# Small early loads gathered on the SP queue and a new hand-fixed instruction order, in a fused long-convolution and SwiGLU kernel

## The chip, the core and the metric

The kernel runs on one core of a Trainium2 chip. The metric is the device time of one execution in microseconds (us); lower is better. Engines are named as in the profile: PE multiplies matrices (PEld loads its weights), DVE and ACT work element by element, POOL does a few tiny operations, and SP only issues transfers. ACT and POOL issue transfers too. All transfers run on the same 16 DMA engines.

## The reference

What is computed, for 2048 rows of 640 channels (the FFN has 1728 hidden columns):

```python
k_shift = sum over t<4 of k_pad[:, t:t+S, :] * shift_k[:, 3-t]     # four-tap filter along the rows
kv  = k_shift * v
y   = irfft(rfft(kv, 2S) * rfft(ssm_k, 2S))[:S] + kv * ssm_D         # causal long convolution per channel
h   = x + layernorm(x) * y                                           # x is A_q
out = h + (silu(layernorm(h) @ w_gate) * (layernorm(h) @ w_up)) @ w_down
```

## The kernel before

**Tiling.** The 2048 rows are cut into four blocks `j` of 512, the channels into two halves `c` of 320. A block's convolution is done as matrix products with transform tables, and the FFN of a block follows when its `h` is complete. Names in the program carry `j`, `c` and a group `G` of the transform:

- `tapm`, `tap0`..`tap3` spread the four filter taps over the partitions. `hl..`/`he..` shift rows of `k` down for the filter, with the shift matrix `shm`. `kvm`, `kva`, `kvv` are the filter's multiplications and additions on DVE.
- `ktr0c` (PE, with the identity `ident`) and `kte0c` transpose the kernel `ssm_k`. For later blocks a transposing transfer `kx` and a shuffle `shk` do it.
- `s1X..`, `s1K..` and their evictions `e1..` are the first transform step of the signal (X) and of the kernel (K). `shX..G`, `shK..G` are transfers that shuffle partitions, `s2..`/`e2..` the second step. For block 0, three of the four transforms are done by one long product with the table `full` instead (function `dense`; here `s2K01`, `s2X00`, `s2X01`). The term with `ssm_D` enters as a product of one partition with the row `drow`, in `s1K00b0` and in `s2K01G0`..`G3`.
- `swB`, `swX`, `swC` are transfers that swap real and imaginary rows; `mr`, `mi` and further products on DVE multiply the spectra. `i2..G` and `e3..` are the first inverse step, `rs..G` the shuffle behind it, `i1..` the second inverse step.
- `q` and `hn` are the two layernorms, `o`, `h` the gate and the residual, `tr`/`te` (block 0) or the transposing transfers `hx` (blocks 1 to 3) turn `h` for the FFN. `gu` are the products with gate and up weights, `dn` those with the down weights.

**Order.** Nothing is scheduled at run time. The program is a list of 1219 operations (`Prog.op`). `Prog.replay` decodes the string `_ORDER`: for each operation an engine and a start value. The start values only sort the operations within each engine's queue, hand out buffers, and set two more things. The first is a count of *fillers* for PE: where the start values leave PE a gap ahead of an operation before the first `gu`, `replay` puts so many dummy products (`P.fill`, line 515 of the profile) into PE's queue, just ahead of that operation:

```python
gap = o.start - end - 0.25
o.lead = max(0, int(gap / 0.083)) if o.start > cold else max(0, int(gap / 0.166))
```

They always run, whether or not PE has to wait there. The second is that a transfer that would be issued more than one unit ahead of its start value is tied to an earlier ACT or DVE operation, so that it isn't issued much too soon. Apart from that every engine works through its queue in order, and an operation waits (by semaphore) for the data that it needs and for the buffer that it writes. An operation that waits holds back all behind it on its engine.

PE's queue before, around two places that matter here (fillers in brackets):

```
... s2K01G2, s2K00G1, [2] s2X00G3, s2X00G0, s2K00G2, s2X01G0, s2X01G1, s2K00G3, s2K01G3, i200G0, i200G1, s2X01G3, s2X01G2 ...
... [18] s2K10G0, [5] s2K10G2, i1010, s2K10G3, [3] s2K10G1, [2] s2X10G3, s1X11b1, [1] s1X11b3, i1011, s1K11b3 ... [19] tr00, [4] i210G1, gu001 ...
```

In code lines: L492 is every ordinary product, L515 the filler, L475/L478 the evictions and L501 the products and sums on DVE, L483 every plain transfer, L777/L778 the layernorm's scaling on DVE and on ACT, L520 and L514 the two memsets that DVE starts with. The second of these, `gpad`, writes the operand of the fillers; `P.warm` is its name in the code.

Of the kernel before, what the change touches and what calls it, by code (L numbers as in the profile page):

```python
# [43 lines left out]
class Prog:  # L44
# [61 lines left out]
    def replay(self, table):  # L106
        n = len(self.ops)
# [6 lines left out]
        for o in sorted(self.ops, key=lambda o: (o.start, o.idx)):  # L114
            for tl in o.tiles:
                if not tl.live:
                    pl = self.pools[tl.pool]
                    pl.free.sort(key=lambda f: f[0])
                    _, tl.base, tl.prev = pl.free.pop(0)
                    tl.live = True  # L120
            q = self.order[o.eng]
            o.pos = len(q)
            q.append(o)
            for tl in o.tiles:
                tl.touch.append(o)
# [211 lines left out]
def bass_sequential_preLN__ssm_conv_h3__swiglu_ffn__prompt_kernel(  # L337
# [31 lines left out]
    with ExitStack() as es:  # L369
# [18 lines left out]
        def V(t, off, n, p0=0, p1=128):  # L388
            return sb[p0:p1, t.base + off:t.base + off + n]
# [115 lines left out]
        def dram(apx, off, pairs):  # L505
            return bass.AP(apx.tensor, apx.offset + off, pairs)
# [580 lines left out]
        def block_j(j):  # L1087
            pb = 1000 * j
            if j == 0:
                load_kv_all(10)  # L1090
                load_full(11)
                tab_piece(2, oS1I, tab_np.shape[1], 30)
                tab_piece(0, 0, oS1K, 40)
                tab_piece(3, oS1K, oW2, 40)
                tab_piece(1, oW2, oS1I, 42)
                dma([(lambda: V(DROW, 0, D, 0, 1), lambda: dram(A_ssm_D, 0, [[D, 1], [1, D]]))], 1, [], [(DROW, 0)], 15, name="drow", eng="act")
            for c in range(2):
                if j:
                    load_kv(j, c, pb + 10 + 20 * c)
# [25 lines left out]

_INFO = None
_ORDER = (
    "c-pO030PBC7A7x`kdOtkhwLj^$i4sx*~tb3LLh`B2#6?%vRJFFindy}X>Bc4i+qk&#tpYBE|t1f9c|UNRIS#PDq2NtYf-0)wiPG1b!_X@nXmV}@0|0_yZ4-X"
    "{`=ntfDi~2h=Dv101AQ+ofrrRg+M_F2!g;<1Ny{!v?eOi0Y3J@fe!=rsX+8CS|?^;*(3A&EKepr$4cnH3*^y$qG1pUjcz^qfDa5b=Fxyafafz&JzxOvH|k+p"
    "=(8~Rb*~`!4F7SPPj&WG6nNCi<CgwBIq>|+A%Bp30KJE^9(sQbQs9FzKnCD}dKOB+A2#)$jCcUbQ|x%=gkRfwUhMv~B=CQfjN%A9Mils~5Pity=Rowo@a|dU"  # L1130
    "co+vj$m1p;{~Lb5?+O5qejC4u1AoXr;0gbtr5>UM{HcBxPD^4UF)JaFm;qS?xdN$z@PP_|2|Ws70+sPCG2cU+z*t~DZ~?%BI`DWb1@<AN4^|IpM7g1#K@Y@)"
    "AR@@Su|2UII0|f!<Hvp!TM8D#uE1YMyoTsS-bT_<+tI^;4FC*U58Vr$4xRxqus$FH{SsuvB4Wd_T~HL*2X%vIW0%D?!M=kB;-<#M!>7Xc!kvimu%BUK#A!rx"
    "{I&SiNG^(xtVeD|DiKo<Y4KI@Juo*s2tNtm5Z{Dyqb{S==t*cMx*ok9U6Y_mIE&em5W=p-9mMWQ>`QFJ+`vx5y+b;OuY!4Fcfhc5)o~}|vf+#2TyQFQBX(C@"
    "ZfpSNMRX#zB9_EAz(=F^qF=!5z#tR*6S5NLB{sw%;RW%%@%xd3P!VJgQjZj)M<wpZl5v%|d)NZpIoxdAQT%OuKH(cefH;x39P1=ZBJL;FkhYSpl9mxS5V0f*"
    "X%gu?$wj_RT1mb|9zu?gH<GuJ&yh<g4U{&DFlkKEJxmvA5<W~_OJBeik&tW{OV8RT=w{Cn9TFWBy&-8%dV%^fC4*X?1X8zAI+J!%ebkw>9NIoAg1(k+rb`*k"
    "%#T=KbB;4;tWxemRu{KlP$BH)mk7=a>y!PW@k|QiJ8l;DF0+<*m-jJG#qSiJN-h_y7nO)5Y$zunTEl*ubCz>lBolukX_QvUa#df;7RvLLe)S%;RdGP^qjIcj"
    "s``j{M~XpqL_SNk1cr&P1PQ1%v@BsV;uNYEGlv2}Yccl|P?$+b7`2)X#qJ?rV|UQMrVr)n5!d1GAb9cT;<d;X$bRI@apSOOuu4oH=5S&S_7>WL5#Z+F|AAxR"
    "C!u@Lqfp0C0rYBg5vm2H#H_{CV>%Ot<6H0(2_1xK37ZmhiPIBz6TeJE5;JgYQVsbS?jZR(B_nA@5}PuT0#Ntk;|Ws2M8dp88TJ#xZNdS9gSeP_g=(hlOxjKf"
    "Qafk>y^B7UzMD>EjN@+QuHgK_q3~Yk>G%qvfe-Q*@vrcmf-M4Ja!Yb4W(9_vP?sP~+?JStos2z<XOl*fwvgtNgQPanb|Q>qrS40rr*Ecdar<xpQB7Qgi^1E7"
    "qlhojjHH`1CH)5)gRZ2N)21;tGgeY5v=F18v5O969$^k;-DY{&vw5TVSNS2{0iIBBn47};fZNNBVHL5KvhJ|P@;>5}@|UqU@#_S?@XrcblVQRm!V$@zCeIbV"  # L1140
    "B1Ve)M0Rnv*e}tf?2(j8Orj=9w`5t$MCmo@dKpnlmyVUzN#{z5vhU?@$XXPO<svypK3P6q{+_&2L02{@<|v8EpR}{J2K5)J3A*iSK`KZ4fo6ZICT)rKXqrkd"
    "*Zfm$PyZ@yo#v+gvSD|IK7(LhX}V~9*DSV1Qa{vvZWwI%HnlN>Yr2@eM9;IVvE&)n*)(>e=@ny#In#XHL^Ch5Fzl~p@*JS+kmrJ9gj4K-dC*xkR-p}-33rq_"
    "I$g8e*`8j{xojM^pIk;BLD|S+ayDppqz_7+lBP(P=(F{Bqt(=7xNahuTg|!nW_%oB0U>$?DPR(s`U<s~UC0^5+0E%>Q#gwmy^K1(fqRZyB)r6=vh2*!%u?q2"
    "%$Y0=dkuf7V3;6IykF2KIL7A-E(kQqPT|<-O}N2J5cMScl8c2`g>Q*);#T2&F<dfEGCk$1l!-E5%7T=ODW9h-lYT3qDoRrLQoZO!(H8L~ak;cz%9Q2FVr2G|"
    "ZL*UxhD<5{n|!3=o?^42P`O4KqpDD?RmG&vSCKTjv|TEh<_pa#?O^R(-Om=4^;=_{xzXBbZLq^LH(GC5-Nsc$hV8fwY45i0rPb5nj55Y1hL`z1%fvY^*e&8n"
    "u1HVI+GHeoSh7q~A&)4WYPw>Iyj{*$1QZVG80j$idBs6hf+|jZUwujmSM5|fR0}kE-3oQT_Pkc7ou<2}hO1xFbm>;70%;Ygp|tk2*z|Sj7=4?$R^Jgl!TISP"
    "!+rgGh7U5_M!$ZG9%EQ-kQ(cZ%QH@7+%jxU?J)8(YBTyXVl5F%lkt?X%v5ZC-+aSrw9T-otxK)ftPWeDv)i)K^_Fdndz{T_Uv9r{w`PvXJeS##>31y5?6ONU"
    "8y)Qqg7c!I)-lF`aypzf&d;6QQF+sq;L33tow=@K&b!VEm*2h0HN%Z?AMy?HHRPSin~`7PyPZES2bD9^+njqRr#g@1qj@p8Tm0Gnw{zbt$O<0ySh6zm+ww`-"
    "R)1Q-)WY6EZBc8{Yk@;SOR+lpldPWLgkVL^{9<H?Txcpd5a=tcEkp-q7P&(ohjSx`BB;88;=`d(SQPo9c6;QrlC08COW9?aC4oU*gGx)w%9b;IiosH@w8T0&"
    "ZG=~wzc=qfJ~7YjUsQO~uPzV;t^_bedy9T#zssR<=W;E)cHZCBH?<}WKXqN|;<PF0RXS&y#9+<Pm@b*OSza(rG2bvR)E(DxObbj4%~DIM^^RqyGsX6{WtW9)"  # L1150
    "t+wuW+;+enX^wq1n{%f--?PGVBI{>Yde-bLcJ^1<f}Hl8#o1T0wK*79o$IDk<?8TU_7FUo9-^l*yC$2K1A4>WCEjg0cf7f|K;9i+W`26!)Vy8!DaF%+C4r=("
    "#^UwG?$9^ICyGuK%?X?haDuJDW5Ic0vNl_nm)@OTr*AXOx7WDVn|f>$?ai*ATulzOv)vYNAD#1#N9XIyD{^<aN4Z<wYqHK{DLk)w1ld32Ov#se|K;W8-p>hm"
    "FXl9PC*-cqZOpr$+nE=W*Xq0FGv^ok=H>hRs|tQBI1%VBP!<x4@ctIR+`rJzEqJlO?c3qI=08yIgFm^jvCv$!uP`gHIB+X~4i*QO1T%wkgWbV<!HVM3#e&e-"
    "(5etDd^WT;bRmQdRfOc>Vc{L&OX1RRFpQ4872X)05Sbm7oe@I`Cz2GQl#GtFM4|^+(qGb1q8+5IY^~fmOkBkoy1MFm#k7j%DxiAQkk_iK%V(F7E7lCYT;5WF"
    "9y)%gYxu_DcZX_fEQ61hpRTU2-Zi*n_@E&NhWLkF8tSS1au~O4OX*K#OUqKrCYCjpvuZZgY#nK+ZK}-}v2TQTWamh3ZCc%~y3O^e4YL}OYuDAf>krm58~zP&"
    "9!w_"
)


# [26 lines left out]
```

## Time and profile before

| | us |
|---|---|
| median of 6 runs | 310.94 |
| lowest and highest | 308.78, 313.08 |
| the profiled execution's own time | 311.48 |
| its span in the profile | 309.6 |

| engine | busy us | share | instructions |
|---|---|---|---|
| PE | 282.8 | 91% | 1765 |
| DVE | 234.7 | 76% | 406 |
| ACT | 186.9 | 60% | 280 |
| POOL | 27.0 | 9% | 34 |

PE's busy time holds the fillers too: 158 of them with 19.47 us. From about 206 us on, only FFN work of blocks 2 and 3 with the rest of block 3's convolution runs, and PE is busy throughout. The first 75 us, before the first `gu`, are different: PE has little real work there and depends on a chain through DVE, ACT and the DMA engines. How to read it: an engine's share over the whole span says little; a stage is bound by the wait that ends last in it.

### The profile page before, as it was taken

Reading aid. Unit: us, or ns where it says so; the run is one execution under the profiler, and the core shown is the slowest. Engines: PE = TensorE matmul, PEld = TensorE weight load, DVE = VectorE, ACT = ScalarE, POOL = GpSimd, SP = SyncE. Lnnn points to the kernel's source line nnn. Section 1 sums busy time; section 2 is a strip of 40 time slices with the busy share of each in tenths; the row PEclk is TensorE's granted clock in tenths of the full one; section 3 lists DMA queues with packets and bytes.
Section 4 is the critical chain, followed back from the end, with each engine's and each line's share of the span. In section 5 each row is a group of like instructions: output and inputs, shape, how many; then the busy total and the mean of one; then the engine's idle time right before and its main releaser. Section 6 shows DMA issues by size and latency. Waiting matters only on the chain.

```text
span 309.6 us, 4974 instructions
## 1 busy us (share of the span) xinstructions
PE 282.8 (91%) x1765; PEld 168.3 (54%) x1780; DVE 234.7 (76%) x406; ACT 186.9 (60%) x280; POOL 27.0 (9%) x34
## 2 busy tenths in 40 slices
PE   7999687779899989997999999979999999999992
PEld 4755365537555546774444566745555675444671
DVE  2896799769899988997999998896889973204222
ACT  3657577748768968674779975646797811250000
POOL 0021201122110011120000110200002010000000
PEclk9999999979999999999999999999999999999998
DMA  6958579669889987588671361445532122000021
GB/s 225 352 197 266 180 237 238 199 199 307 242 282 281 298 258 274 161 241 223 190 253 42 122 212 71 131 147 203 200 114 78 46 51 76 2 0 0 2 85 43
DMA packets 53116, 52.09 MB, mean 168 GB/s; under 512 B 21202, under 2 KB 46163, under 8 KB 53092
## 3 DMA queue, kind: packets, MB, share of 16 engines
q1 hardware_dynamic: 50274, 44.06, 44.4%
q0 software_dynamic: 1808, 6.93, 8.0%
q10 hardware_dynamic: 1010, 0.79, 0.8%
q8 instruction: 14, 0.23, 0.3%
q14 instruction: 10, 0.08, 0.1%
HBM read 19.00 MB, written 2.62 MB: 70 GB/s over the span
## 4 chain that ended last, share of the span: by engine, by line
PE 67%; DMA 11%; ACT 8%; DVE 6%; issue 3%; SPq 3%; POOL 0%; ACTq 0%; DVEq 0%
PE ps L492 62%; DMA sb<-sb 9%; ACT sb L475 5%; DVE sb L501 4%; PE ps L515 4%; SPq L483 2%; DMA sb<-in_A_ssm_D_dram 2%; ACT sb L478 1%; ACT sb L778 1%; ACT sb L790 1%; DVE stt L755 1%; DVE sb L777 0%; PE ps L624 0%; POOL stt L768 0%; SPq L981 0%
## 5 line engine op out<-in xcount | busy, mean ns | idle before, releaser
L492 PE MATMUL ps<-sb 128*128 128x320 bf16 (+3 forms) x1113 | 207.3, 336 | 2.6 <-DVE sb L501 1.6
L501 DVE TENSOR_TENSOR sb<-sb 128x1280 bf16<-128x1280 bf16 (+2 forms) x238 | 173.9, 767 | 16.5 <-ACT sb L475 4.8
L492 PEld LDWEIGHTS ps<-sb 128*128 128x128 bf16 (+2 forms) x1128 | 108.7, 98 | 83.1 <-issue 5.2
L475 ACT ACTIVATE sb<-ps 128x640 bf16<-128x640 f32 x131 | 88.7, 712 | 39.3 <-PE ps L492 38.6
L492 PE MATMUL ps<-sb,tab 128*128 128x320 bf16 x450 | 78.3, 304 | 11.2 <-DMA sb<-sb 7.2
L492 PEld LDWEIGHTS ps<-sb,tab 128*128 128x128 f16 x450 | 42.4, 99 | 39.2 <-DMA sb<-sb 8.1
L501 DVE TENSOR_TENSOR sb<-ps,sb 128x640 bf16<-128x640 f32 (+3 forms) x34 | 29.2, 858 | 42.4 <-PE ps L492 40.9
L1034 ACT ACTIVATE sb<-ps 128x1024 bf16<-128x1024 f32 (+2 forms) x32 | 29.3, 916 | 23.7 <-PE ps L492 23.6
L778 ACT ACTIVATE sb<-sb,stt 128x320 bf16<-128x320 bf16 (+1 forms) x34 | 24.0, 728 | 7.2 <-DVE stt L770 4.8
L478 ACT ACTIVATE sb<-ps 128x640 bf16<-128x640 f32 x31 | 21.0, 705 | 11.3 <-PE ps L492 11.3
L515 PE MATMUL ps<-sb 128*128 128x192 bf16 x158 | 19.5, 271 | 7.1 <-ACT sb L475 4.2
L755 DVE BATCH_NORM_STATS2 stt<-sb 128x6 f32<-128x320 bf16 x48 | 22.3, 483 | 0.2
L1050 ACT ACTIVATE sb<-ps 128x1024 bf16<-128x1024 f32 x18 | 18.4, 1024 | 5.6 <-PE ps L492 4.7
L515 PEld LDWEIGHTS ps<-sb 128*128 128x128 bf16 x158 | 14.3, 107 | 12.5 <-ACT sb L475 7.3
L768 POOL TENSOR_TENSOR stt<-stt 128x2 f32<-128x2 f32 (+1 forms) x10 | 11.4, 1138 | 53.2 <-DVE stt L766 42.7
L476 DVE CAST sb<-ps 128x640 bf16<-128x640 f32 (+1 forms) x8 | 6.2, 779 | 7.3 <-PE ps L492 7.3
L804 POOL TENSOR_TENSOR stt<-stt 128x4 f32<-128x4 f32 x2 | 2.6, 1298 | 77.9 <-DVE stt L802 77.9
L790 ACT ACTIVATE sb<-sb 128x640 bf16<-128x640 bf16 x8 | 6.0, 744 | 2.1 <-DMA sb<-in_A_q_dram 2.1
L797 ACT ACTIVATE sb<-sb,stt 128x640 bf16<-128x640 bf16 x8 | 6.6, 832 | 0.0
L777 DVE TENSOR_SCALAR sb<-sb,stt 128x320 bf16<-128x320 bf16 (+1 forms) x14 | 5.5, 395 | 0.9 <-DMA sb<-sb 0.5
L483 POOL DMA_DIRECT2D sb<-in_B_w_down_dram x3 | 2.1, 699 | 33.5 <-DVE sb L501 29.5
L483 POOL DMA_DIRECT2D sb<-in_A_k_dram x2 | 2.1, 1028 | 26.4 <-DVE stt L759 26.4
(30 smaller groups left out, 33.7 us busy)
## 6 DMA issues: line engine op xcount, KB each, us to landing
sb<-sb SPq DMA_DIRECT2D x144, 160.0 KB, 2.3
out_dram<-sb SPq DMA_DIRECT2D x16, 160.0 KB, 1.9
sb<-in_A_k_dram SPq DMA_DIRECT2D x4, 560.0 KB, 4.4
sb<-in_A_q_dram SPq DMA_DIRECT2D x3, 640.0 KB, 4.7
sb<-sb SPq DMA_DIRECT2D x24, 80.0 KB, 3.2
sb<-in_A_v_dram POOLq DMA_DIRECT2D x4, 320.0 KB, 4.6
sb<-in_A_k_dram POOLq DMA_DIRECT2D x2, 560.0 KB, 4.6
sb<-cst_full SPq DMA_DIRECT2D x1, 1024.0 KB, 8.8
```

Source lines behind the costliest of these rows:

```text
L475: fns = {"act": lambda a: a.activation(out=dst(), in_=src(), func=ACTF.Copy), "dve": lambda v: v.tensor_copy(out=dst(), in_=src())}
L478: fns = {"act": lambda a: a.activation(out=dst(), in_=src(), func=ACTF.Copy, scale=scale), "dve": lambda v: v.tensor_scalar(out=dst(), in0 ...
L483: fns = [(lambda g, d=d, s=s: g.dma_start(d(), s())) for d, s in subs]
L492: return lambda t: t.matmul(o(), l(), r(), start=st, stop=sp)
L501: return lambda v: v.tensor_tensor(out=o(), in0=a(), in1=b_(), op=op)
L515: P.fill = lambda t, pt: t.matmul(B32(pt, 1, 192), V(GUT, 13 * 512 + 256, 128), V(GUT, 13 * 512, 192), start=True, stop=True)
L755: vec(dve1(CW, False), lambda v: v.bn_stats(st6(l, j, b, c), V(xt, b * D + c * CW, CW)), [(xt, (b, c))], [(ST, ("s", j % 2, b, c))], prio, ...
L768: P.op({"pool": 0.95}, lambda g: g.tensor_tensor(out=y, in0=va, in1=stt[:, 288:288 + hi - lo], op=ALU.pow), c1 + [(ST, "half")], c3, prio, ...
L778: "act": lambda a: a.activation(out=dst(), in_=src(), func=ACTF.Identity, scale=rs(l, j, b), bias=tmv(l, j, 3)[:, b:b + 1])},
L790: P.op({"act": act_c(D) + 0.22}, lambda a, b=b, jt=jt: a.activation(out=V(jt, 0, D), in_=V(xt, b * D, D), func=ACTF.Copy, accum_out=tmv(l, ...
L1034: P.op({"act": act_c(n)}, lambda a: a.activation(out=dst(), in_=src(), func=ACTF.Silu), rd, wr, -1000, name=f"si{j}{i}")
L1050: P.op({"act": act_c(1024)}, lambda a: a.activation(out=V(ut, 0, 1024), in_=B32x2(u, 512), func=ACTF.Copy), [(u, 0), (u, 1)], [(ut, 0)], - ...
```

## The change

It has four parts. No operation is added or removed, except the dummy products.

1. **Loads.** `ident`, `shm`, `drow` (both times ACT before) and the first table piece `tab0` are issued by SP.
2. **`replay`** moves `gpad` to the head of DVE's queue, in front of `wpad`.
3. **A new `_ORDER`.** Every engine's queue is sorted anew, and 57 operations change their engine.
4. With it the count of fillers goes from 158 to 212.

```diff
@@ Prog.replay
+        q = self.order[self.warm.eng]
+        q.remove(self.warm)
+        q.insert(0, self.warm)
+        for i, o in enumerate(q):
+            o.pos = i
@@ the loads
-        dma([(lambda: V(IDN, 0, 128), ...)], 33, [], [(IDN, 0)], -2990, eng="act", name="ident")
-        dma([(lambda: V(SHM, 0, 128), ...)], 33, [], [(SHM, 0)], -2991, eng="act", name="shm")
+        dma([(lambda: V(IDN, 0, 128), ...)], 33, [], [(IDN, 0)], -2990, eng="sp", name="ident")
+        dma([(lambda: V(SHM, 0, 128), ...)], 33, [], [(SHM, 0)], -2991, eng="sp", name="shm")
...
-                tab_piece(0, 0, oS1K, 40)
+                tab_piece(0, 0, oS1K, 40, "sp")
...
-                dma([(lambda: V(DROW, 0, D, 0, 1), ...)], 1, [], [(DROW, 0)], 15, name="drow", eng="act")
+                dma([(lambda: V(DROW, 0, D, 0, 1), ...)], 1, [], [(DROW, 0)], 15, name="drow", eng="sp")
@@ the order
-    "c-pO030PBC7A7x`kdOtkhwLj^$i4sx*~tb3LLh..."
+    "c-pO#2UwHW8po6G3y_da_TGyuNJ0o?k_{w4AS93=..."
```

Decoded, the queues differ as follows.

The transfers at the start, each queue in its order:

```
            before                                             after
SP    taps, kin0, kraw00, x0, kraw01, full, vin0,     shm, taps, kin0, kraw00, ident, tab0, kraw01, full,
      tab1, kx10, shk10, swB010, shK00G3, swB000,     drow, x0, kx10, shK00G1, kin10, swB000, vin10, x1,
      swB001, swB011, rs00G1, kin11 ...               swB010, shk10, swB001, rs00G0, kin11, swB011 ...
ACT   shm, tab0, ident, drow, shK00G1, shK00G0,       vin0, shK00G0, shK00G2, tab2, shK00G3, rs00G1
      shK00G2, rs00G0
POOL  kin10, tab2, x1, vin10, tab3, vin11, kin20,     tab1, tab3, vin11, kin20, wg3, gul0, gul1, wd9,
      wg3, wg9, wu0, wu3, wd0, wd9, wdl, vin30,       wdl, vin30, x3
      vin31
```

SP's queue where block 0's second half is finished:

```
before  ... swX100, shK10G0, rs01G2, shK10G2, rs01G3, shK10G3, shK10G1, shk11, swB101, swX101, swB100 ...
after   ... swX100, shK10G0, rs01G2, shK10G3, shK10G1, rs01G3, shK10G2, wg9, shk11, swX101, swB100 ...
```

SP's queue where block 2's kernel is shuffled:

```
before  ... swX201, shK21G0, hx11, shK21G3, shK21G1, hx10, hx13, hx12, shX21G1 ...
after   ... swX201, hx10, shK21G1, hx11, shK21G0, rs20G1, hx12, st03, hx13, shX21G1 ...
```

PE's queue at the two places shown above:

```
after   ... [5] s2K00G3, s2K00G2, s2K01G2, s2X01G1, s2X01G0, s2X01G3, i200G0, i200G1, [21] s1X10b3, s2X01G2 ...
after   ... [15] i1010, s2K10G1, s2K10G2, [5] i1011, s2K10G3, [19] s1K11b1 ... [8] tr00, i210G1, gu000 ...
```

Where the fillers stand:

| PE's queue | before | after |
|---|---|---|
| up to the first `s2K01` product | 45 | 54 |
| from there to `i200G0` | 3 | 7 |
| from `i200G0` to the first `gu` | 110 | 151 |
| later | 0 | 0 |

The PE operations up to the first `s2K01` product are the same before and after, but for one product pair (`hl12`) that comes into this stretch; up to `i200G0` they are the same but for `s2X01G3`, which now stands before it; and up to the first `gu` they are the same.

On DVE and ACT, five of block 0's eight `q` scalings, `hn01`, `hn03` and the eviction `e300G2` move from ACT to DVE, `te01` and `he11` from DVE to ACT; later blocks exchange a dozen more in both directions. Between the product `mi0000` and the scaling `hn02`, DVE's queue holds 69 operations before and 79 after, both included but for `mi0000`.

## The prediction

> **What bounds the kernel now.** I read the page's engine and slice rows first, then busy time by stage, then the fillers of each stage, then the chain of work that ended last. The engine and slice rows:
>
> ```profile
> PE 282.8 (91%) x1765; PEld 168.3 (54%) x1780; DVE 234.7 (76%) x406; ACT 186.9 (60%) x280; POOL 27.0 (9%) x34
> ...
> PE   7999687779899989997999999979999999999992
> ...
> PEclk9999999979999999999999999999999999999998
> ```
>
> PE is the bound on average, and from slice 27 on in fact. But 91% includes dummy products, and slices 4 to 8 are thin. So I cut the span into five stages: A up to the first `s2K01` product, B to `i200G0`, C to the first `gu`, D to 205.88 us, E the rest. First PE, DVE and ACT, then the fillers (L515) alone:
>
> ```profile
> 0.00:15.49 15.49, 13.35 (x94) 9.64 (x95) 8.79 (x15) 8.20 (x11) 0.40 (x5) 1.00 0.88 289
> 15.49:33.53 18.04, 15.38 (x102) 8.96 (x101) 13.73 (x25) 10.96 (x17) 3.10 (x5) 1.00 0.69 238
> 33.53:74.65 41.12, 32.44 (x252) 21.31 (x253) 34.57 (x69) 29.01 (x46) 8.93 (x9) 0.96 0.75 220
> 74.65:205.88 131.23, 124.16 (x767) 74.07 (x776) 122.67 (x210) 98.00 (x147) 11.58 (x12) 1.00 0.67 204
> 205.88:303.75 97.87, 97.44 (x553) 54.31 (x558) 54.09 (x90) 40.77 (x61) 2.96 (x3) 1.00 0.21 73
> ...
> 0.00:15.49 15.49, 7.08 (x46) 5.53 (x46) 1.00 0.88 289
> 15.49:33.53 18.04, 0.41 (x3) 0.11 (x2) 1.00 0.69 238
> 33.53:74.65 41.12, 11.98 (x110) 8.68 (x110) 0.96 0.75 220
> ```
>
> The first figure is the stage's length, the second PE's busy time, the fourth DVE's. E has 0.43 us of idle PE: nothing to win. D has 7.07. In C only 32.44 - 11.98 = 20.46 us of 41.12 are real products, 8.68 us are idle. C is not PE's stage; a chain of DVE, ACT, SP and transfers sets it. The chain shows which transfers:
>
> ```profile
> 9.65 4.69 DMA sb<-in_A_ssm_D_dram
> ...
> 26.52 6.10 DMA sb<-sb
> 32.65 0.84 DVE sb L501
> ...
> 58.76 4.89 DMA sb<-sb
> ...
> 110.05 5.12 DMA sb<-sb
> ...
> 136.66 4.59 DMA sb<-sb
> ```
>
> These are `drow`, `swB000`, `shK10G1`, `shX20G1` and `shK21G1`: 4.6 to 6.1 us each, where the page's median shuffle takes 2.3:
>
> ```profile
> sb<-sb SPq DMA_DIRECT2D x144, 160.0 KB, 2.3
> ```
>
> PE waits 2.14 us for `i200G0` (`swB000`, then one DVE product), 2.43 for `s2K10G1`, 1.3 for `s2X20G1` and 1.75 for `s2K21G1`.
>
> **Part 1: the loads.** SP gets four more issues, some 0.4 us each (rows of SP's queue at the start: 0.35 to 0.48). They stand ahead of `x0` and `kx10`, which nobody needs before 11 us. In exchange `vin0` goes to ACT at once. Up to the end of `full` the same bytes move as before (`vin0`'s 640 KB in place of `x0`'s), so `full` still lands at about 4.14 + 8.8 = 12.9 us by its row; `kin0` and `kraw00` come later by what `vin0` took behind `full`, 14.5 - 12.9 = 1.6 us, so at 6.9 and 9.1. PE reaches their first users at 8.2 (1.2, 21 fillers 3.6, four `tapm` 2.2, 7 fillers 1.2) and, after four `hl` and 3 fillers, 10.7: hidden; without the fillers there it would cost up to 1.6.
>
> `drow` is where rule and trace part. [...] The row says that it took 4.69 us, to 14.34, together with `vin0`: the short queue got no turn. By the row it moves from 14.34 to about 13.0 (bounds: 7, if it passed all, 14.5 if it lands with `x0`). I take the row, 13.0: PE's 0.50 us of idle time in A goes, but PE is not there earlier (next part), so the loads alone are worth nothing.
>
> **Part 2: `gpad` first.** The fillers start after one DVE memset of 0.28 us instead of two: 1.2 instead of 1.64 us.
>
> **Parts 3 and 4 by stage**, lengths before and after.
>
> *A, 15.49.* PE's own queue is its length. Starts at 1.2; real products 13.35 - 7.08 = 6.27; `hl12` comes in, 0.5 at the slow clock; 54 fillers: 28 at 2.74/16 = 0.171 us, 9 at 2.31/16 = 0.144, 17 at 0.099, together 7.8; idle 0.3. Sum 16.1: **+0.6** (-0.4 to +1.6, `kraw00`).
>
> *B, 18.04.* Real products 14.97 - 0.27 (`hl12`) + 1.09 (`s2X01G3` now precedes `i200G0`) = 15.79; 7 fillers at 0.109, 0.76. Idle 2.66, of which 2.14 was `swB000`. SP issued it behind `shk10` (4 issues), `swB010` and `shK00G3`, and beside `x1` and `vin10`; now it stands behind `kin10` alone and ahead of these loads. PE has made its inputs at 16.1 + three `s2K01` at 1.8 + 1.1 + 0.55 = 23.2, ACT with evictions of 0.7 queued ahead of them at about 25; issued by 25.6, even at the old 6.10 it lands by 31.7, and with the DVE product at 32.5 it is within PE's 33.2. So 0.52 stays. Sum 17.07: **-1.0** (none: +1.2).
>
> *C, 41.12.* Real products 20.46, less 1.09 (moved to B), less the slow clock. The profile's clock rows:
>
> ```profile
> 62.29:65.70 3.41, 1.50 (x10) 0.76 (x11) 1.24 (x4) 1.52 (x3) 0.00 (x0) 1.00 0.70 241
> 65.70:69.11 3.41, 3.41 (x15) 1.60 (x14) 2.72 (x10) 1.70 (x3) 1.46 (x2) 0.50 0.60 159
> ```
>
> After a window with 1.50 us of PE work the next ran at half clock: 1.7 us lost. [...] Here the longest gap was 2.43. [...] I take the row: 17.67. Fillers 151 at 0.109: 16.4. Idle 8.68, less 2.43: `shK10G1` was the last of six shuffles on SP and met `wg3`; now it is issued before `rs01G3`, so when `i1010` can run it has landed, and `i1011` no longer stands behind `s2X10G3` and two `s1X11` products. That leaves 6.25; 41 more fillers, 4.5 us, may lie in waits that were idle; DVE, below, leaves room for 2.0 at most (17.67 + 16.4 + 6.25 is 40.3, its floor 38.3), and I take 1.5, leaving 4.7 (4.2 to 8.7). Sum 38.8: **-2.3**. What is late next is DVE. Its queue from `mi0000` to `hn02` grows from 69 to 79 operations: `e300G2` 0.82, `bn` 0.49, two `hn` 0.9, five `q` 1.4, four small 0.8, less 0.7; so 34.57 + 3.7 = 38.3. C can't be much below that, so I don't take more. ACT loses as much and has room (29.01).
>
> *D, 131.23.* `shK21G1` stood behind `shK21G0` (0.56), the transpose `hx11` (1.29) and `shK21G3` (0.59); now only `hx10` precedes it, while `shK21G0`, used just before, comes third: 1.4 of the 1.75 goes. `shX20G1` has as much PE work ahead as before (3 us): stays. PE's 1.59 at 205.88 is ended by DVE: stays. `wu0`, `wu3`, `wg9`, `wd0` go from POOL to SP at 0.6 us each, issued earlier; no use of them was waited for. Sum **-1.4** (-3.4 to +1).
>
> *E*: 0.
>
> **Sum**: +0.6 - 1.0 - 2.3 - 1.4 = -4.1, so 311.48 becomes 307.4 in the profiled execution. Against the median of the runs, 310.94, that is **306.8**. One per cent, 3.1 us, is about what a measurement of this kernel can tell from no change.
>
> **Rivals.**
>
> *Same: a collision replaces the one removed.* POOL now issues `kin20` and `wg3` back to back, over 1 MB, ahead of `rs01G2` and `rs01G3`, which lead to `i1010`. If those take 4.9 instead of 2.3, C gets 2.6 back and the half clock's 1.7: +0.2, 311.1. For it: DMA share 0.75 in C, and `wg3` did this before. Against: 15 fillers ahead of `i1010` keep PE busy.
>
> *Slower: the fillers are paid in full.* They run whether or not PE waits. 54 more cost 5.5 us, over 5 of them in B and C. If no wait there goes and the half clock stays, B is 15.79 + 0.76 + 2.66 = 19.2 and C 19.37 + 16.4 + 8.68 = 44.5: with A's 0.6 that is +5.1, **316.0**. It decides (slower by 1%) from where less than 2 us of waits is saved. For it: already before, fillers are followed by waits, as if they stood in the wrong places. Against: the transfers that ended the longest waits are those moved forward.
>
> *More*: all idle time in C that fillers can cover goes, and D's waits too: A -0.4, B -1.0, C down to DVE's 38.3 (-2.8), D -3.4: 303.3.
>
> *The loads do nothing* by themselves is my own assumption above; it alone decides no sign.
>
> **Chances.** Forecast 0.50 (it spreads, so 0.12 of it lies within 1%), same 0.19, slower 0.21, more 0.10. Faster by over 1%: 0.38 + 0.10 = 0.48; within 1%: 0.31; slower: 0.21. Range 301.5 to 314: down to the "more" case with a margin, up through "same" and into the slower one. The likeliest's own: 303 to 310.
>
> **What would show it.** Right: the first `s2K01` product at 15.5 to 16.5; `drow` landed near 13; `i200G0` at 32.5 to 33.5 with no wait over 0.5; no half clock near 66; the first `gu` at 70 to 73; `s2K21G1` waiting under 0.6; 212 fillers with about 25 us. Wrong: the first `gu` at 75 or later with more filler and no less idle time (the slower rival), or an early `gu` whose gain D gives back in waits for weights or shuffles.

## The result, and the profile after

The changed kernel takes 309.37 us (median of 29 runs, 306.45 to 311.97), the kernel before, run beside it, 312.37 us (64 runs). The ratio is 0.9914, 95% interval 0.9892 to 0.9936; a second series of the same two (e1 below) gave 0.989 (0.9859 to 0.9921). Medians are of all runs; the ratios count only the fast ones, those within 1.5% of the fastest of their kernel. So about 3 us are gained, where 4.1 were forecast, and not where they were forecast. The profiled execution of after took 310.75 us, 0.73 less than that of before; one lies above its median and the other below, so 2 us of the gain can't be seen in this pair of profiles.

First the page of after, engine and slice rows:

```profile
PE 287.9 (93%) x1819; PEld 173.8 (56%) x1834; DVE 235.9 (76%) x413; ACT 184.4 (60%) x273; POOL 22.6 (7%) x29
...
PE   8899988587899998998999999999999999999993
...
PEclk9799999879999999999999999999999999999999
```

PE has 54 matmuls more, all fillers. The half clock that stood in slice 8 of before is still there, now over two slices, and a second one has come in slice 1. Then the same table by stage: length, PE, PEld, DVE, ACT, POOL, granted clock, DMA share. The last row holds what were D and E (131.23 + 97.87 = 229.10 us before). Below the dots are the fillers alone (L520 now):

```profile
0.00:16.88 16.88, 14.39 (x105) 10.31 (x105) 10.04 (x15) 8.00 (x11) 1.15 (x7) 0.90 0.95 261
16.88:34.04 17.16, 16.70 (x113) 10.04 (x114) 15.39 (x27) 10.05 (x16) 0.00 (x0) 1.00 0.72 235
34.04:78.75 44.71, 35.31 (x287) 25.42 (x286) 35.49 (x75) 26.09 (x40) 7.09 (x7) 0.92 0.75 222
78.75:303.77 225.02, 221.51 (x1319) 128.02 (x1332) 174.14 (x299) 140.27 (x208) 14.35 (x15) 1.00 0.48 149
...
0.00:16.88 16.88, 7.21 (x54) 5.80 (x54) 0.90 0.95 261
34.04:78.75 44.71, 17.03 (x151) 13.22 (x151) 0.92 0.75 222
```

A grew by 1.4 us, B shrank by 0.9, C grew by 3.6 (44.71 instead of 41.12), and all behind it shrank by 4.1. In this pair of profiles that adds up to nothing: the last product ends at 303.77 us after and at 303.75 before. The 0.7 us by which the profiled execution of after is shorter lie behind the last product. Part of them is the end of the program, where SP waits once for every semaphore that a transfer has used. When the last output has landed, 43 semaphore instructions of SP are left in before and 36 in after, and the span ends 2.96 and 2.52 us later. It ends 2.46 to 2.53 us later in all profiles with after's order up to the first `gu`, 2.96 to 3.02 in all with before's. No step of the prediction counted that.

C has no less idle PE than before: 44.71 - 35.31 = 9.40 us, against 8.68, although its fillers went from 11.98 to 17.03 us. The chain of work that ended last, by start, length and what, shows where they lie:

```profile
1.61 6.80 DMA sb<-in_A_k_dram
...
34.60 0.71 ACT sb L483
35.32 0.05 issue
35.36 1.91 PE ps L520 x21
...
52.06 6.65 DMA sb<-sb
...
63.04 1.46 PE ps L520 x8
...
65.04 1.78 PE ps L520 x15
...
70.62 1.74 PE ps L520 x19
```

Between 35 and 77 us fifteen pieces of this chain are fillers, 13.9 us of the 17.0. In before they were ten, 8.6 of 12.0. The pattern, as at 35 us: an eviction on ACT ends, 0.05 us later fillers start, and the product stands behind them. And 52.06 is the shuffle `shK10G0`, issued between `kin20` (51.23) and `wg3` (52.18): 6.65 us, with PE waiting for `s2K10G0`.

### The profile page after: what moved, and what is told of

Read it like the earlier page. It is cut to its first block, busy times and chain, and to the rows that moved or that the text cites. A ratio compares the mean times of both kernels' runs of the same rounds, so it can differ in the third digit from the quotient of the medians.

```text
span 308.9 us, 5073 instructions
## 1 busy us (share of the span) xinstructions
PE 287.9 (93%) x1819; PEld 173.8 (56%) x1834; DVE 235.9 (76%) x413; ACT 184.4 (60%) x273; POOL 22.6 (7%) x29
## 3 DMA queue, kind: packets, MB, share of 16 engines
q0 software_dynamic: 960, 3.41, 4.0%
## 4 chain that ended last, share of the span: by engine, by line
PE 75%; DMA 8%; ACT 7%; DVE 5%; issue 2%; SPq 1%; ACTq 0%
PE ps L497 69%; DMA sb<-sb 5%; PE ps L520 5%; ACT sb L480 5%; DVE sb L506 4%; DMA sb<-in_A_k_dram 2%; SPq L488 1%; ACT sb L1039 1%; DVE stt L760 1%; ACT sb L483 0%; ACT L1039 0%; PE ps L993 0%; PE ps L629 0%; ACT sb L1055 0%; DVE sb L484 0%
## 5 line engine op out<-in xcount | busy, mean ns | idle before, releaser
L497 PEld LDWEIGHTS ps<-sb 128*128 128x128 bf16 (+3 forms) x1128 | 109.0, 98 | 83.9 <-issue 4.3
L480 ACT ACTIVATE sb<-ps 128x640 bf16<-128x640 f32 (+1 forms) x134 | 90.7, 714 | 44.6 <-PE ps L497 42.0
L520 PE MATMUL ps<-sb 128*128 128x192 bf16 x212 | 25.1, 272 | 7.6 <-ACT sb L480 6.0
L520 PEld LDWEIGHTS ps<-sb 128*128 128x128 bf16 x212 | 19.6, 108 | 14.7 <-ACT sb L480 11.2
L483 ACT ACTIVATE sb<-ps 128x640 bf16<-128x640 f32 x29 | 19.5, 702 | 10.6 <-PE ps L497 10.5
L783 ACT ACTIVATE sb<-sb,stt 128x320 bf16<-128x320 bf16 (+1 forms) x26 | 19.1, 754 | 3.9 <-DVE stt L775 3.2
L481 DVE CAST sb<-ps 128x640 bf16<-128x640 f32 x6 | 4.8, 820 | 4.9 <-PE ps L497 4.7
L782 DVE TENSOR_SCALAR sb<-sb,stt 128x320 bf16<-128x320 bf16 (+1 forms) x22 | 7.9, 379 | 0.1
L764 DVE BATCH_NORM_AGGREGATE stt<-stt 128x2 f32<-128x12 f32 x24 | 4.3, 195 | 0.0
L488 POOL DMA_DIRECT2D tab<-cst_tab x2 | 1.3, 634 | 36.9 <-ACT sb L480 26.5
```

The costliest lines, as they stand in the source:

```text
L480: fns = {"act": lambda a: a.activation(out=dst(), in_=src(), func=ACTF.Copy), "dve": lambda v: v.tensor_copy(out=dst(), in_=src())}
L483: fns = {"act": lambda a: a.activation(out=dst(), in_=src(), func=ACTF.Copy, scale=scale), "dve": lambda v: v.tensor_scalar(out=dst(), in0 ...
L497: return lambda t: t.matmul(o(), l(), r(), start=st, stop=sp)
L782: "dve": lambda v: v.tensor_scalar(out=dst(), in0=src(), scalar1=tmv(l, j, 5)[:, b:b + 1], scalar2=rs(l, j, b), op0=ALU.add, op1=ALU.mult),
L783: "act": lambda a: a.activation(out=dst(), in_=src(), func=ACTF.Identity, scale=rs(l, j, b), bias=tmv(l, j, 3)[:, b:b + 1])},
```

## The experiments

Each was timed against the kernel before on the same chip; the ratio is to that. "First `gu`" is the end of the first `gu` product in the profile of that kernel, "behind it" the time from there to the last product's end. e17 has two runs only, and so no ratio.

| kernel | fillers | first `s2K01` starts | `i200G0` ends | first `gu` | behind it | DVE operations done at first `gu` | median us | ratio (95%) |
|---|---|---|---|---|---|---|---|---|
| before | 158 | 15.49 | 34.26 | 75.38 | 228.35 | 107 | 312.37 | 1 |
| after | 212 | 16.88 | 34.58 | 79.30 | 224.48 | 114 | 309.37 | 0.9914 (0.9892-0.9936) |
| e1 after again | 212 | 16.70 | 34.39 | 78.00 | 225.08 | 114 | 308.59 | 0.989 (0.9859-0.9921) |
| e2 after, 28 cut | 184 | 16.54 | 34.24 | 76.08 | 225.98 | 114 | 307.98 | 0.9879 (0.9818-0.994) |
| e3 after, `wg3` late | 212 | 16.58 | 34.28 | 75.19 | 224.62 | 114 | 306.54 | 0.9857 (0.9808-0.9907) |
| e4 before, then after | 158 | 14.54 | 32.13 | 75.91 | 227.56 | 107 | 311.22 | 0.9965 (0.9933-0.9997) |
| e5 e3, 63 cut | 149 | 17.00 | 34.69 | 74.34 | 224.44 | 114 | 306.55 | 0.9846 (0.9792-0.9899) |
| e6 e3, 151 cut | 61 | 16.49 | 34.18 | 72.15 | 224.32 | 114 | 305.42 | 0.978 (0.9719-0.9841) |
| e7 before, loads on SP | 158 | 17.01 | 33.63 | 74.47 | 227.98 | 107 | 312.48 | 1.0043 (1.0012-1.0073) |
| e8 e5, `vin0` later | 133 | 15.38 | 33.91 | 72.91 | 228.43 | 112 | 308.34 | 0.9867 (0.9815-0.992) |
| e9 after, 151 cut | 61 | 17.72 | 35.42 | 71.89 | 224.68 | 111 | 303.77 | 0.9759 (0.9719-0.9799) |
| e10 before, 110 cut | 48 | 14.86 | 33.23 | 72.18 | 228.77 | 108 | 306.68 | 0.9866 (0.9822-0.9911) |
| e11 after, then before | 212 | 18.59 | 36.29 | 78.51 | 225.28 | 115 | 312.81 | 0.9992 (0.996-1.0025) |
| e12 e6, `vin0`, `wdl` | 45 | 17.11 | 35.08 | 76.30 | 226.76 | 115 | 307.58 | 0.9816 (0.9764-0.9868) |
| e13 before, `vin` later | 158 | 15.61 | 34.54 | 76.03 | 226.95 | 107 | 311.38 | 1.0004 (0.9973-1.0035) |
| e14 before, `shK21G1` | 158 | 15.55 | 33.72 | 75.98 | 227.52 | 107 | 311.03 | 0.9981 (0.994-1.0022) |
| e15 after, 191 cut | 21 | 14.39 | 31.92 | 69.20 | 226.81 | 111 | 302.20 | 0.9724 (0.9675-0.9774) |
| e16 e15, `wdl` early | 21 | 14.11 | 31.64 | 69.95 | 225.21 | 114 | 302.73 | 0.9692 (0.9638-0.9745) |
| e17 as e11 | 212 | 17.21 | 34.90 | 75.77 | 226.28 | 115 | 312.06 | none |
| e18 before, 73 cut | 85 | 15.68 | 33.33 | 70.94 | 229.26 | 107 | 308.46 | 0.9914 (0.9883-0.9946) |

Stage marks of one profile scatter by a us or two; the ratios are the firmer column.

### Is the split typical, and what are fillers worth? (e1, e2, e9, e10, e15)

e1 is the changed kernel again.

> The changed kernel once more, to learn whether the profile of it shown above is typical: its first gu started at 78.75 us, 3.9 us later than before, and everything behind it took 225.0 us instead of 229.1. If this split belongs to the order, the second profile shows the first gu at 77.5 to 80, the half clock near 60 again, and a time of 309.0 to 309.8. If the late transfers near 52 us were chance, the first gu starts at 74 to 77 and the time is one to three us shorter in that execution.

The split belongs to the order: 78.00, then 225.08 us.

Fillers are set by each operation's `lead`. e2 sets three of them to 0:

```
         for o in self.order["pe"]:
+            if o.name in ("s2X10G3", "i1010", "i1011"):
+                o.lead = 0
```

> The changed kernel without the 8, 15 and 5 fillers ahead of s2X10G3, i1010 and i1011 (28 of 212; the chain of after charges 1.46 and 1.78 us to them). Theory F (fillers are paid: transfers had made PE late, so the planned gaps no longer exist): the first gu comes 2.5 to 3 us earlier, near 76, and the time falls to 307 to 308. Theory T (the transfers set these products, the fillers lie in waits): PE waits instead of running fillers, the first gu stays within 1 us of 78.7, the time within 0.5 us of the changed kernel.

The first `gu` came at 76.08, 1.9 us before e1 and 3.2 before after: theory F. The ratio can't be told from that of e1.

e9 takes all 151 of C away (from `s1X10b3` on), e10 the 110 of before (from `i200G0` on):

```
+        on = False
         for o in self.order["pe"]:
+            on = on or o.name == "s1X10b3"
+            if on:
+                o.lead = 0
```

> The changed kernel without the 151 fillers between i200G0 and the first gu, wg3 where the change put it, directly behind kin20. With wg3 moved as well the first gu ended at 72.15 us and the ratio was 0.978. Theory F (fillers are most of the loss): first gu at 72.5 to 74, ratio 0.979 to 0.984. Theory T (the collision is most of it): shK10G0 takes over 6 us as in after, s2K10G0 waits 3 us or more, first gu at 75 to 77, ratio 0.985 to 0.99.

> The kernel before without its 110 fillers between i200G0 and the first gu; all else as before. Theory F: those too are paid; the first gu ends 2 to 4 us before 75.38, the time falls to 308.5 to 310 (ratio 0.988 to 0.995). Theory W (before, the stage waits for shuffles with or without fillers): first gu at 74.5 to 75.5, ratio 0.996 to 1.004.

Theory F in both, and past its own figure: 0.9759 after, 0.9866 before. In each order the fillers of C cost about 1.3%, 4 us. Without their 17.03 us C of after, from the end of `i200G0` to that of the first `gu`, fell from 44.72 to 36.47: half of them came back. Of the other half, 6.4 us went into the real products (busy 24.67 us instead of 18.29) and 2.4 into waits (11.80 us instead of 9.40). The clock did what it was feared to do: its granted share in this stretch was 0.86 instead of 0.92. Engine and clock rows of e9:

```profile
PE 278.8 (92%) x1668; PEld 160.9 (53%) x1683; DVE 235.7 (78%) x413; ACT 184.6 (61%) x273; POOL 22.6 (7%) x29
...
PEclk9999999579999999999999999999999999999998
```

More of C is at half speed than in after, and the kernel is the faster for it all the same.

e15 leaves only the 21 fillers ahead of the first product:

```
+        for o in self.order["pe"]:
+            if o.name != "tapm":
+                o.lead = 0
```

> The changed kernel with only the 21 fillers ahead of the first product left (191 cut: 151 in C, 33 in A, 7 in B). Theory F: the 33 and 7 are paid as well in part; the first s2K01 product starts at 14.5 to 15.5 instead of 16.7 and the ratio is 0.970 to 0.975, under the 0.9759 with the 151 cut. Theory C (near the start they hold the clock up): half clock from 8 to 15 us, the first s2K01 product at 16.5 or later, ratio 0.976 to 0.982.

Theory F again: first `s2K01` at 14.39, 2.5 us before after's, and 302.20 us. Its ratio and that of e9 overlap; that the 40 in A and B cost something is shown by the mark alone.

### What does `wg3` behind `kin20` cost? (e3, e5, e6)

```
+        for o in self.ops:
+            if o.name == "wg3":
+                o.start = 54.5        # was 47.38; behind shK10G2
```

> The changed kernel with the weight load wg3 no longer directly behind kin20 on POOL but after shK10G2 (seven shuffles later). Theory T (collision): shK10G0, which took 6.65 us from issue to landing, takes 3 to 5; the wait of 2.9 us for s2K10G0 falls under 1, the first gu comes 2 to 3 us earlier, the time is 307 to 308. Theory F (fillers): only the wait goes, the fillers behind it stay in PE's queue and i1010 is reached little earlier; the first gu moves by under 1 us, the time by under 0.5 us.

The chain of e3 at the same two places:

```profile
51.76 5.22 DMA sb<-sb
...
61.47 1.24 PE ps L524 x15
...
66.51 1.74 PE ps L524 x19
```

`shK10G0` takes 5.22 instead of 6.65 us, the four shuffles issued between 55.8 and 57.8 take 2.1 to 2.2 each instead of 2.3 to 3.0. The first `gu` came at 75.19, 2.8 to 4.1 us earlier, and this profile has no half clock in C:

```profile
PEclk9799999999999999999999999999999999999999
```

Theory T, for the marks; the ratio, 0.9857, overlaps with e1's. The product behind the 15 fillers still waits for them.

> The changed kernel with wg3 behind shK10G2 and, besides, without the 63 fillers from s2K10G0 to the first gu (149 of 212 stay). With wg3 moved alone the first gu ended at 75.19 us and everything behind it took 224.6 us. Theory F (these fillers lie on PE's path, since PE and ACT's evictions take turns there and a filler comes between them): the first gu ends at 71.5 to 73, the time is 303.5 to 305.5. Theory T (the shuffles of the next half, shk11 above all, landed at 66.3 us, and the evictions set the end of the stage): the first gu stays at 74.5 or later, 306 to 307. Theory G (the lead is given back behind the first gu, because the loads of weights come no earlier): the first gu ends near 72, but 226 to 228 us follow, 305.5 to 307.

First `gu` 74.34, ratio 0.9846: nearer to theory T. Of 63 fillers cut on top of `wg3`, 0.9 us came back; the profile has half clock where e3 had none.

> The same, but with no filler at all between i200G0 and the first gu (61 of 212 stay). Theory F: PE is nowhere slowed by a dummy product, the first gu ends at 70 to 72, the time is 302 to 304.5. Theory C (the fillers hold the clock): with some 20 us of real products in 40 us several windows of 3.41 us at half clock appear, each worth up to 1.7 us; the granted clock of the runs falls from 0.99 to under 0.985, the first gu ends no earlier than with 63 cut, the time is the same or higher.

72.15 and 0.978, granted clock 0.9725 on average in its six runs: the clock fell as theory C said, the time fell as theory F said. It can't be told from e9 (0.9759), where `wg3` stands as in after: with the fillers gone `shK10G0` was issued 0.2 us ahead of `kin20` in e9, instead of 0.8 behind it, and took 3.18 us. The collision was a matter of the fillers as much as of the place of `wg3`.

### The loads at the start (e7, e8, e12)

e7 is part 1 alone: before, with `shm`, `taps`, `kin0`, `kraw00`, `ident`, `tab0`, `kraw01`, `full`, `drow`, `x0` on SP and `vin0` on ACT at the times of after:

```
+            if o.name in at:
+                o.eng, o.start = ("act" if o.name == "vin0" else "sp"), at[o.name]
```

> Part 1 alone: the kernel before with shm, ident, tab0 and drow on SP and vin0 on ACT at once, in the order of after; all else as before. By the prediction the loads alone are worth nothing (311.5 to 312.5 here). By the profile of after they cost: kin0 lands near 8.2 us instead of 5.3, since vin0 now stands ahead of it, hl01 is 1.5 to 2 us later, kraw01 and full land 0.6 to 1.1 us later, so the first s2K01 product starts near 16.5 instead of 15.49; 312 to 313.5 if it is carried to the end, 312 if later waits swallow it.

`kin0` landed at 8.20, PE waited for it and the first `s2K01` started at 17.01. The ratio is 1.0043 and its interval excludes 1: the loads cost about 1.3 us (0.4 to 2.3 by the interval).

e8 issues `vin0` at 1.61 us instead of 0.74 and drops the fillers ahead of `hl01`, `ktr00` and `ktr01`; e12 does so on top of e6 and moves `wdl`.

> The changed kernel with wg3 moved and 63 fillers cut, and vin0 issued behind kin0 instead of ahead of it, without the 16 fillers ahead of hl01, ktr00 and ktr01. kin0 should land near 5.5 us, the first s2K01 product start near 15.2 instead of 16.6. If the start is carried through, the time is 1 to 1.4 us under that with vin0 as in after, 302.5 to 304.5; if the next stages wait for x0, the evictions and the shuffles anyway, it is the same within 0.5 us.

> What the runs point to, together: wg3 behind shK10G2, no filler between i200G0 and the first gu, vin0 behind kin0 with no fillers ahead of hl01, ktr00 and ktr01, and the last weight load wdl issued directly behind wd9 (it landed at 130 us in two runs and PE waited 1.8 us for it). If the parts add up: first gu at 70.5 to 71.5, 224.5 us behind it, ratio 0.972 to 0.978. If the earlier start is swallowed as it was in part before: 0.978 as with wg3 and the 151 fillers alone.

Both missed: 0.9867 where e5 had 0.9846, 0.9816 where e6 had 0.978 (the intervals overlap in both pairs, so a loss isn't shown either). `kin0` landed at 6.9 us and A ended earlier in e8 (15.38), but `kx10`, issued near 7 us, took 14.4 and 15.4 us to land instead of 10.1 to 11.6 in e3, e5 and e6, `tab1` 11.0 and 11.7 instead of 5.7 to 7.6: the delay moved on to the next loads. Besides, e8's profile has a half clock at 212 us that e5's has not.

### Where the gain behind the first `gu` comes from (e4, e11, e13, e14, e17, e18)

e4 takes before's order for everything that before starts ahead of its first `gu`, and after's for the rest; e11 and e17 the other way round:

```
+        late = [(0.01 * int(s), o.idx, self.ENG[e]) for o, e, s in zip(self.ops, raw2[:n], ...) if o.start >= 62.63]
+        for r, (s, i, e) in enumerate(sorted(late)):
+            o.eng, o.start = e, max(62.63 + 0.0001 * r, s - 3.08)
```

> All operations that the order of before starts ahead of its first gu stand as before, fillers and loads included; all others follow in the order of after. Theory D (the order behind the first gu brings the gain by itself): first gu at 74.3 to 75.3 as before, 225 us behind it as after, so 306.5 to 307.5, faster than both. Rival H (head start: in after the late first gu gives DVE, SP and the transfers a lead over PE, and that lead is what saves waits later): behind the first gu 228 to 229 us, so 310 to 311.5.

> The order of after up to its first gu, the order of before behind it. Theory D (the order behind the first gu brings the gain by moving shK21G1, rs21G3 and hx22 forward): the waits for s2K21G1, i1210 and gu230 (1.9, 0.9 and 1.5 us before) return, 228 to 229 us follow the first gu, which ends at 77 to 79.5; 312 to 313.5, slower than before. Rival H (the late first gu gives SP and DVE a lead): these waits stay away, 224.5 to 226 us follow, 308.5 to 309.8 as after.

> The order of after up to the first gu and that of before behind it, once more, for a second profile: the first showed 225.3 us behind the first gu, as after, but its time was 2 us under the median of its runs, 312.81. Rival H (DVE's lead, 115 operations done at the first gu instead of 107, shortens what follows, whatever the order there): again 225 to 226 us, with a first gu at 79 to 81. Theory D (the order behind the first gu counts too): 227 to 229 us, with waits for s2K21G1, i1210 or gu230 of over 1 us each.

Neither half does it alone: 0.9965 and 0.9992, where both together give 0.989. In the profiles 227.56 us follow the first `gu` in e4, 225.28 and 226.28 in e11 and e17, whose back is that of before. PE's waits behind the first `gu` in before, then in e17 (what waits, for what: us in all, times, longest):

```profile
PE ps L492 <- DMA sb<-sb: 4.4, 4, 1.8
PE ps L492 <- DVE sb L501: 1.9, 2, 1.6
```

```profile
PE ps L503 <- DMA sb<-sb: 2.8, 3, 1.8
...
PE ps L503 <- DVE sb L512: 0.3, 1, 0.3
```

In after nothing of this size is left:

```profile
PE ps L497 <- DMA sb<-sb: 1.2, 2, 0.9
PE ps L497 <- ACT sb L483: 0.9, 1, 0.9
```

PE's idle time behind the first `gu` is 7.47 us in before and 3.50 in after, while its busy time there is the same (220.9 and 221.0 us): the gain in D is idle time and nothing else. The waits of before for `s2K21G1` (1.75), `gu230` (1.59) and `i1210` (0.72) are gone, those for `s2X20G1` and `s2K11G0` are 0.7 shorter together; new are 0.87 for `gu120` and 0.38 for `s2X31G1`.

The 1.8 is `shK21G1` in both before and e17. The 1.6 "for DVE" of before is gone. It never was DVE: the trace of PE's own queue has a wait of 1.84 us, from 203.56, on the transfer `hx22`, which landed at 205.37; DVE's part was done by 203.08. In e17 `hx22` took 2.40 us, in before 4.15, at the same place in the same queue.

e13 and e14 take the wait for `s2K21G1` away in before, in two ways:

```
+            if o.name in at:          # e13: vin30 124.9, vin31 170.5;  e14: shK21G1 118.6
+                o.start = at[o.name]
```

> The kernel before with two loads moved on POOL, vin30 (328 KB) behind the shuffle shK21G1 and hx10, vin31 behind rs21G3, rs21G2 and swB300, as the change has them; no SP order touched. In before they were issued within 0.4 and 1.5 us ahead of these shuffles, which took 4.59 and 4.31 us where neighbours took 2.1. Theory V (a load issued just ahead slows the shuffle): shK21G1 takes 2.2 to 2.7 us, s2K21G1 waits under 0.5 us instead of 1.7, i1210 under 0.4; 2 to 2.5 us less behind the first gu, ratio 0.992 to 0.995. Theory O (the place in SP's queue is what counts, as the prediction had it): shK21G1 still lands near 140.5 or later, s2K21G1 waits 1.2 us or more, ratio 0.997 to 1.003.

> The kernel before with the one shuffle shK21G1 moved ahead of shK21G0, hx11 and shK21G3 on SP; loads untouched. Theory O: it is issued 2.5 us earlier, lands by 137 and the wait of 1.7 us for s2K21G1 goes, though shK21G0, used next, may now be the late one (0 to 0.5); ratio 0.994 to 0.997. Theory V: it lands early too, since vin30 is issued after it; then shK21G3 and hx11 meet vin30 without PE waiting; the same ratio. Both expect the wait to go; if it does not, neither holds. i1210 and gu230 keep their waits of 0.9 and 1.5 us by both.

Both nearly succeed in that, and the ratios show no gain. PE's waits from 139 to 147 us in before, in e13, in e14:

```profile
PE ps L492 <- DMA sb<-sb: 1.8, 1, 1.8
```

```profile
PE ps L497 <- DVE sb L506: 2.0, 1, 2.0
PE ps L497 <- DMA sb<-sb: 0.2, 1, 0.2
```

```profile
PE ps L497 <- DVE sb L506: 1.5, 1, 1.5
```

The shuffle landed at 139.77 and 136.52 us instead of 141.25. Five products later PE came to `gu101` and stood there as long. Again the page names DVE, done at 142.49 in e13; PE's wait ended at 144.36, when `hx12`, the transposed input, had landed (144.32; 143.56 in e14). In before the two waits lay one behind the other and only the first was to be seen. PE's idle time ahead of `i1210`, 0.72 us in before, was gone in e13, where `vin31` had moved away, and 0.36 in e14; `gu230` kept its 1.6 in both.

Why does a shuffle take 2.1 us here and over 4 there? The page of before has a queue that no line of the kernel feeds (name, transfers, MB, share):

```profile
q8 instruction: 14, 0.23, 0.3%
```

Fourteen transfers of 16 KB, in the traces one for about every 122 matmuls with their weight loads. From the queue's name and this spacing the author takes them for fetches of PE's code, and they are called code fetches below; the traces show only their times, sizes and spacing. In before three of them start at 136.59, 184.76 and 203.08 us, while `shK21G1`, `rs21G2` and `hx22` are under way; in after, with 54 fillers more and another order, at 133.82, 175.60 and 195.15. In before, e7, e13 and e14 one starts 1.8 to 1.9 us after the issue of `hx22`, which then takes 4.13 to 4.19 us; in e2 and e12 one starts 0.2 us after it, 2.93 and 2.94; in the other fourteen none falls between its issue and its landing, and it takes 2.36 to 2.46. Over the shuffles and transposes of 160 KB behind 80 us in all twenty profiles, against a base of 2.1 us (2.4 for transposes):

| under way beside it | number | later by, mean us | later by over 1 us |
|---|---|---|---|
| nothing | 366 | 0.06 | 1% |
| a code fetch | 76 | 1.14 | 63% |
| a larger transfer, mostly a load | 835 | 0.68 | 26% |
| both | 121 | 1.50 | 79% |

This is a comparison and not an experiment, and the numbers of the four groups shift by some tens with where "beside" is taken to begin; their order does not.

e18 moves the fetches in before by cutting 73 of its fillers:

```
+            if on:
+                o.lead = 0
+            if o.name == "s2K10G0":
+                break
```

> The kernel before without the first 73 of its 110 fillers between i200G0 and the first gu (up to s2K10G0). The traces show 14 transfers of 16 KB on the queue that the page calls q8 instruction, one for about every 130 matmuls with their weight loads. In before three of them start at 136.59, 184.76 and 203.08 us, while the shuffles shK21G1, rs21G3 and hx22 are under way, for which PE waits. 73 matmuls fewer move this grid 55 matmuls forward, almost as the 54 added fillers did in after. Theory I (the gain behind the first gu is that shift of the code fetches): fetches near 131, 151, 173 and 192 us; the wait of 1.8 us for hx22 goes, rs21G3 takes under 3.2 us instead of 4.31; shK21G1 may stay late by the load vin30; 225.5 to 227 us behind the first gu; ratio 0.980 to 0.986, no slower than with all 110 cut (0.9866), though 37 more fillers run. Theory L (DVE's lead, 107 against 114 operations done at the first gu, brings that gain): DVE has done 107 or 108, 228 to 229 us follow the first gu, PE waits 1.5 to 1.9 us for hx22; ratio 0.989 to 0.993.

A half answer. The fetches came at 128.76, 146.94, 171.84 and 194.42, `hx22` took 2.46 us and PE waited 0.6 instead of 1.8 for it, with DVE at 107 operations: that wait was the fetch's. But `shK21G1` (4.53) and `rs21G3` (4.02) stayed late beside the loads `vin30` and `vin31`, and 229.26 us followed; the ratio, 0.9914, is theory L's. That doesn't decide for L: PE's idle time behind the first `gu` fell from 7.47 to 5.35 us, and its products took 3.0 us more (223.91 instead of 220.88), with a half clock from 138.58 us that no theory had. So each wait has its cause, but how much of the 4 us DVE's lead brings is still open.

e16 is e15 with the last weight load issued directly behind `wd9`:

> The changed kernel with only the first 21 fillers, and the small weight load wdl issued directly behind wd9 on POOL. With the fillers cut alone the ratio was 0.9724, and in its profile PE waited 1.8 us for wdl (dn0310) and 224.3 to 226.8 us followed the first gu. If that wait is at home in most executions: the wait goes, 224.5 to 225.5 us follow, ratio 0.967 to 0.970. If it is chance: 0.970 to 0.975.

The wait for it went, 225.21 us follow the first `gu`. 0.9692 can't be told from e15's 0.9724. e15 and e16 beat both before and after.

## Why the prediction was right or wrong, point by point

**A, +0.6 forecast, +1.4.** `drow` landed at 12.65, forecast 13.0; the trace's row held (in before its one packet of 1280 bytes began at 13.57 us, 3.92 us after the issue). The failed step is "the loads alone are worth nothing". It let `vin0` delay `kin0` by 1.6 us, to 6.9; `kin0` landed at 8.40 (5.30 before), and at 6.5 to 8.8 in the twelve kernels that issued `vin0` first, at 7.6 or later in ten of them. PE waited 0.7 us for it and then 0.6 for ACT, and the fillers behind it ran all the same. A half clock from 8.00 to 11.41 us, which no step had, came on top. e7, which has no half clock there, gives the loads' price: 0.43%.

**B, -1.0 forecast, -0.9.** Right, by its own step: `swB000` landed at 28.50 and `i200G0` didn't wait.

**C, -2.3 forecast, +3.6.** Real products were rightly sized (18.3, partly at half clock, for 17.7), the fillers nearly (17.03 for 16.4). The failed term is the idle time: 4.7 forecast, 9.40 found. The step said that 1.5 us of the new fillers "may lie in waits that were idle" and that 2.43 us of wait would go besides. The code says why nothing lay there:

```
                    early = {... for p in sorted([self.warm] + pt.prev, ...) if p.eng != "pe"}
                    ...  prog.append(("w", p.sem, p.semval))
                    prog.extend([("f", ...)] * o.lead)
```

Fillers write the buffer of the product that they precede, so PE first waits until ACT has emptied it, and only then runs them. The time in which PE waits for ACT for that buffer can't be filled. PE's waits in C of after:

```profile
PE ps L520 <- ACT sb L480: 5.3, 10, 0.8
PE ps L497 <- DMA sb<-sb: 2.9, 1, 2.9
```

Ten of them, 5.3 us, are waits of the fillers themselves; the 2.9 is `s2K10G0`, which waits for `shK10G0`, where 2.43 for `shK10G1` was to go. Where the product's inputs are there by then, a filler delays it and the next eviction: PE and ACT take turns with the two buffers of a pool, so the filler's time passes into the chain. e9 and e10 show it in both orders, net of the slower clock: about half of the fillers' time in C came back in e9. DVE's floor, 38.3, which the step leaned on, never bound: its work in C came to 35.49.

**The clock.** The step took the row of before, where a window with 1.50 us of work and 2.43 us as its longest gap was followed by half speed. In after a window with 0.51 us of work and a wait of 2.9 us is followed by it too. Three windows of after, PE's busy time second, the clock third from the end:

```profile
55.75:59.16 3.41, 0.51 (x5) 0.33 (x5) 3.41 (x6) 0.95 (x2) 0.00 (x0) 1.00 0.86 307
59.16:62.57 3.41, 2.83 (x14) 1.38 (x11) 1.23 (x3) 2.23 (x4) 0.00 (x0) 0.51 0.61 150
62.57:65.98 3.41, 2.94 (x18) 2.57 (x19) 0.00 (x0) 1.72 (x3) 0.00 (x0) 0.50 0.71 237
```

The twenty profiles have 26 such stretches between 30 us and PE's last product: in the 3.41 us ahead of each PE was busy for 2.0 us at most, and the longest gap was 3.1. But the row doesn't hold everywhere. In before the window from 31.57 to 34.99 us holds 1.46 us of work and full speed follows, and the half clock of after at 8.00 us follows a window with 3.18 us of work; eleven profiles have such a one near 8 us, and its cause is open. What the step had wrong is that the half clock of C would go: `shK10G0` took over from `shK10G1` as the late shuffle, with 6.65 us.

**D, -1.4 forecast, -4.1.** A gain, three times as large, and mostly by other steps. The forecast step, `shK21G1` earlier on SP, does bring it in 2.46 us after its issue; alone no gain shows (e14), since `hx12` was nearly as late, and in after 0.87 us of waiting for `gu120` came in its place. Two more waits went, which the working let stand or didn't count: `i1210` (0.7), whose shuffles no longer have `vin31` beside them, and `gu230` (1.6). For that the sentence that failed is "PE's 1.59 at 205.88 is ended by DVE: stays". It took the name in the profile at its word; the awaited transfer was `hx22`, delayed by a code fetch that started at 203.08 us in before; in after it came at 195.15. The end of the program behind E, which had no term, gave 0.4. Not settled: e11's ratio is 1% above e1's, while its and e17's profiles show a short stretch behind the first `gu`; both were taken of executions under the median of their runs, so what the usual ones lose wasn't seen.

**The rivals.** *Same*: its collision came, but struck `shK10G0`, not `rs01G2` and `rs01G3`. *Slower*: its mechanism, fillers paid in full, was the nearer one for C, and its 44.5 us for C is what came (44.71), in part by luck: a new wait of 2.9 us stands for the old one of 2.43, and e9 got back only half of the fillers' time. Its sign was wrong, since it let D be. The faster sign of the forecast came by luck too: a term of -2.3 came out at +3.6, one of +0.6 at +1.4 and one of -1.4 at -4.1. With B's -0.9 these add up to nothing in the profiles. They were taken of an execution below the median of before and one above that of after, so where the runs save the rest of the 3 us is not shown.

## What to carry to other kernels

Ask of each dummy product what it waits for before it runs. Here the fillers stood behind the wait for the buffer of the product that they precede (5.3 us in C of after) and covered none of it, and about half of their 17.03 us came back when they were cut (e9). When a transfer takes twice its usual time (`shK10G0` 6.65 us in after, 3.18 in e9; `hx22` 4.15 in before, 2.46 in e18), look for the load or the code fetch that ran beside it, and before a removed wait is counted as gain, for the transfer that is just as late behind it (`hx12` in e13 and e14).

## What was not expected of the hardware

- Shuffles with a code fetch (16 KB) beside them came 1.14 us later on average, as the table above shows, and for `hx22` 1.7 to 1.8. With 73 matmuls cut these fetches moved in all that follows (171.84 and 194.42 us in e18; 161.31, 184.76 and 203.08 in before): part of what an edit gains or loses can be that.
- Half clock is cheaper here than what kept it away. e9's six runs had a mean granted clock of 0.983 and e15's 0.975, e1's 22 runs 0.990; e9 and e15 were 1.3% and 1.7% faster. In the runs of before and of e1 a higher clock went with a shorter time: 0.01 of clock with some 1.0 us over the 34 runs of before that e1's ratio counts (a loose relation, correlation -0.3), with 1.3 over its 17 of e1 (-0.6).
- SP's issue of the transposing load `kx10` took 5.53 us in after and 1.91 in before; SP issued nothing else meanwhile, and its next issue came at 18.56 us in after.
